# Two heads' score products issued in turn, their two PSUM banks held as one tile, in an attention, MoE and MLP kernel

## The chip, the cores and the metric

The kernel runs on one core of one Trainium2 chip. The metric is the device time of one execution in microseconds (us). The core has a matrix engine (TensorE, "PE" in the profile; its weight loads are listed apart as "PEld"), a vector engine (DVE), a scalar engine (ACT), GpSimd (POOL), and DMA queues that SyncE (SP) feeds.

## The reference

Causal attention with a decay goes into a mixture of four dense experts and then into an MLP with a gate.

```python
# q, k, v: (2, 8, 576, 64), f: (2, 8, 576)
scores = scale * np.matmul(q, k.transpose(0, 1, 3, 2))
cum = np.cumsum(np.log(np.clip(f, 0.0001, 1.0)), axis=-1)
scores = np.where(causal, -1e9, scores + cum[:, :, :, None] - cum[:, :, None, :])
attn = softmax(scores)                       # max, exp, sum + 1e-9
x = (attn @ v), laid out as (1152, 512)
# MoE: D = 512, E = 4, F = 1024
out += p[:, e:e + 1] * (np.maximum(x @ w1[e], 0.0) @ w2[e])   # for each e
# MLP: d_ff = 2048
h = x @ w_in
return (h * sigmoid(1.702 * h)) @ w_out
```

## The kernel before

The 1152 tokens (2 batches of 576) are cut into four chunks for the attention: 256 and 320 tokens of batch 0 (chunks 0 and 1), the same of batch 1 (chunks 2 and 3). Twelve weight blocks follow, eight of the MoE and four of the MLP. Every block is two layers (`emit_l1`, `emit_l2`, the `m` products in the traces). Nearly every product is made three times, from a rounded high part and a remainder: high by high, low by high, high by low.

The attention is cut into units, and a unit passes through scores (PE), maximum (DVE), exponential (ACT), division by the sum (DVE and POOL), transposes (PE, tile `t`), product with the values (PE, tile `x`). `emit_scores` makes the scores, and there are three kinds:

- "Plain" units, chunk 0 alone: one head, two query tiles, each one product of 65 rows (`s<-kd,qd`). There are 8 units with 16 tiles in all.
- Pair units: the same 128 queries of two heads. Head 0 lies in partitions 0 to 63 and head 1 in partitions 64 to 127 of the same tiles, so a product of either contracts over 64 rows (form `64*128` in the profile). Each head has three products and a PSUM bank of its own. There are 24 such units, of 128, 256, 384 or 512 keys.
- The tail units, 64 queries of both heads stacked over all 128 rows and 576 keys in two halves of 288: 8 units, two banks each.

The scores go into the PSUM pool `ps_s`, which holds two tiles of one bank each. `emit_max` (line 420) reads them on DVE, one or two instructions for each bank, and a bank comes free when its last reading is done. `ps_t` (three banks) holds `t` and `x`, `ps_m` (three banks) the layers' products; together they fill the eight banks.

The order of the instructions on an engine is fixed when the kernel is built: a scheduler works through the program by priorities and an estimate of time, and each engine then runs its list in that order. `tc.keep_in_program_order(ins)` holds an instruction in the order in which the program gives it. The main loop alternates layers (`m`) with calls of `pull()`, which emit the attention by units. When the attention's buffers come free, `begin_late` opens the buffers into which the MLP's 64-bit weights are loaded (`mst`, line 192), and DVE converts them (`cvt`, `wf`, `cvd`, lines 212 to 228).

Of the kernel before, what the change touches and what calls it, by code (L numbers as in the profile page):

```python
# [7 lines left out]
F32 = mybir.dt.float32  # L8
# [4 lines left out]
PSUM = bass.MemoryType.PSUM  # L13
# [19 lines left out]
def attn_moe_mlp(ctx: ExitStack, tc: tile.TileContext, qk0, qk1, qk2, v0, vp, fg, dp, wa_moe, wb_moe, wa_mlp, wb_mlp, outT):  # L33
# [6 lines left out]
    nc = tc.nc  # L40

    def pool(name, bufs, space=None, scope=ctx):
        kw = {} if space is None else {"space": space}
        return scope.enter_context(tc.tile_pool(name=name, bufs=bufs, **kw))
# [35 lines left out]
    att_scope = ctx.enter_context(ExitStack())  # L80
# [17 lines left out]
        p = late["ps"] if late and ps_n[0] % 8 < 5 else ps_m  # L98
        return p.tile([128, 512], F32, tag="m", name="m")

    ps_s = pool("ps_s", 2, PSUM, scope=att_scope)
    ps_t = pool("ps_t", 3, PSUM, scope=att_scope)

    tri = ac.tile([128, 128], F32, name="tri")
# [184 lines left out]
    def plain(c):  # L289


        return c == 0
# [74 lines left out]
    def emit_scores(c, u):  # L367


        hs, tiles = u  # L370
        out = []
        for q0 in tiles:
            w = min(q0 + 128, S)
            if plain(c):
                st = heads[c, hs[0]]
                mm = [(0, w, [(st["qd"][:, q0:q0 + 128], st["kd"][:, :w])])]
            else:
                p = pass_of[c]
                hi, lo = (pairs[p, hs[0]][k] for k in ("hi", "lo"))
                if q0 < 512:  # L380
                    o = S + 128 + q0 - p[2]
                    zs = [(0, w, slice(64 * g, 64 * g + 64)) for g in range(2)]
                else:
                    o = S
                    zs = [(a, z, slice(0, 128)) for a, z in ((0, 288), (288, S))]
                mm = [(a, z, [(l[r, o:o + 128], k[r, a:z]) for l, k in ((hi, hi), (lo, hi), (hi, lo))]) for a, z, r in zs]
            pts = []
            for a, z, _ in mm:
                pts.append(ps_s.tile([128, 512], F32, tag="s", name="s"))
                out.append((q0, w, a, z, pts[-1]))  # L390
            n = len(mm[0][2])
            for i in range(n):
                for pt, (a, z, lr) in zip(pts, mm):
                    nc.tensor.matmul(pt[:, :z - a], lhsT=lr[i][0], rhs=lr[i][1], start=i == 0, stop=i == n - 1)  # L394
        raw_s[c, u] = out

    def emit_max(c, u):
# [111 lines left out]
    def attention():  # L509
# [8 lines left out]
        first = {k: i for k, i in first.items() if k[0][2] or k[0][1]}  # L518
        nxt = list(first)
        per_unit = dict(scores=emit_scores, max=emit_max, exp=emit_exp, norm=emit_norm, tr=emit_tr)  # L520
        by_last = dict(pv=emit_pv, x2=emit_x2)
        names = sorted(STAGES, key=lambda k: -STAGES[k])
# [185 lines left out]
    for i, (kind, v_, b, c) in enumerate(seq):  # L708
# [6 lines left out]
        for g in range(4):  # L715
            ev = early[g] if i == 0 else (emit_l1 if kind == 1 else emit_l2)(v_, b, c, g)
            n = 0
            if nxt:
                j, cc = nxt[0]
                left = (j - i) * 4 - g  # L720
                n = max(0, -(-(due[cc] - pulled[0]) // left))
# [75 lines left out]
```

## Time and profile before

| what | us |
|---|---|
| median of three runs (736.33, 737.4, 1168.98) | 737.4 |
| the profiled execution, whole | 737.77 |
| its span, first to last instruction | 736.1 |
| PE busy, share of the span | 715.6, 97% |
| DVE busy | 460.2, 63% |
| ACT busy | 268.4, 36% |
| POOL busy | 277.6, 38% |

The profile is of one execution. A matmul's listed duration reaches from its start to a modelled end and overlaps with its successors, so what a matmul costs PE is read from start to start: in a timeline, the difference of the first column from one row to the next.

### The profile page before, as it was taken

To read this page: it belongs to the slowest core of one execution; us is meant where nothing else is said; L and a number is where in the kernel's file an instruction comes from. 1 tells how busy PE (TensorE), PEld (TensorE's weight loads), DVE (VectorE), ACT (ScalarE), POOL (GpSimd) and SP (SyncE) were. 2 spreads that over 40 slices of the span, in tenths; PEclk is the share of its full clock that TensorE was granted. 3 is DMA by queue.
4 is the path that set the end of the run, shared out by engine and by line. 5 is a ranking of instruction groups with operands and counts; after the bars stand their busy time and mean duration, and the time that the engine had idled before them with its cause. 6 is when DMAs were issued, how large, how long until landed. Compare 5 with 4: busy or idle time off the path is not lost.

```text
span 736.1 us, 11924 instructions
## 1 busy us (share of the span) xinstructions
PE 715.6 (97%) x4488; PEld 674.9 (92%) x4488; DVE 460.2 (63%) x1023; ACT 268.4 (36%) x629; POOL 277.6 (38%) x345
## 2 busy tenths in 40 slices
PE   4999999999999999999999999999999999999998
PEld 3576788888899999999998999999999999999997
DVE  4785666575758999999999633445972124424422
ACT  4564554566542233222211221223354433323420
POOL 4886974653432022233232433232462222222220
PEclk9999999999999999999999999999999999999999
DMA  8776534332216464464443301000100000000012
GB/s 290 222 233 208 159 123 132 90 103 86 73 51 216 144 194 149 148 183 117 130 144 115 86 24 35 1 1 1 58 0 1 1 1 1 1 0 1 1 44 86
DMA packets 29496, 67.23 MB, mean 91 GB/s; under 512 B 3032, under 2 KB 4576, under 8 KB 29440
## 3 DMA queue, kind: packets, MB, share of 16 engines
q1 hardware_dynamic: 29392, 66.44, 28.9%
q8 instruction: 35, 0.57, 0.3%
q14 instruction: 21, 0.17, 0.1%
q10 hardware_dynamic: 48, 0.05, 0.0%
HBM read 64.05 MB, written 2.41 MB: 90 GB/s over the span
## 4 chain that ended last, share of the span: by engine, by line
PE 75%; DVE 13%; DMA 5%; issue 3%; POOL 3%; ACT 0%; ACTq 0%; DVEq 0%; POOLq 0%
PE m L604 32%; PE m L560 31%; PE s L394 5%; PE t L461 3%; PE x L491 3%; DVE wlo L163 3%; DMA mst<-in_wa_mlp_dram 2%; DMA mst<-in_wb_mlp_dram 2%; DVE cvd L226 1%; DVE wf L220 1%; DVE cvt L214 1%; DVE tmp L618 1%; DVE cvt L212 1%; DVE hl L587 1%; DVE wf L228 1%
## 5 line engine op out<-in xcount | busy, mean ns | idle before, releaser
L620 POOL TENSOR_TENSOR acc<-acc,tmp 128x384 f32<-128x384 f32 (+3 forms) x112 | 111.2, 1004 | 248.9 <-DVE tmp L618 238.0
L604 PE MATMUL m<-hh,wlo 128*128 128x384 f32 (+2 forms) x640 | 128.0, 320 | 1.4 <-DVE wlo L163 1.3
L604 PE MATMUL m<-hh,whi 128*128 128x384 f32 (+2 forms) x640 | 129.1, 321 | 0.0
L604 PE MATMUL m<-hl,whi 128*128 128x384 f32 (+2 forms) x640 | 127.7, 320 | 0.0
L560 PE MATMUL m<-xh,whi 128*128 128x384 f32 (+2 forms) x624 | 126.1, 322 | 0.4 <-DVE hl L587 0.2
L560 PE MATMUL m<-xl,whi 128*128 128x384 f32 (+2 forms) x624 | 126.2, 321 | 0.0
L560 PE MATMUL m<-xh,wlo 128*128 128x384 f32 (+2 forms) x624 | 126.2, 321 | 0.0
L53 ACT ACTIVATE whi<-wst 128x512 fp32r<-128x512 f32 x103 | 64.9, 631 | 119.8 <-PE m L560 58.0
L163 DVE TENSOR_TENSOR wlo<-wst,whi 128x512 fp32r<-128x512 f32 x112 | 93.3, 836 | 24.3 <-ACT whi L53 13.7
L604 PEld LDWEIGHTS m<-hh,wlo 128*128 128x128 f32 x640 | 105.6, 188 | 3.2 <-DVE wlo L163 2.4
L604 PEld LDWEIGHTS m<-hh,whi 128*128 128x128 f32 x640 | 105.8, 188 | 1.7 <-issue 0.7
L560 PEld LDWEIGHTS m<-xh,whi 128*128 128x128 f32 x624 | 103.1, 188 | 3.7 <-issue 1.7
L604 PEld LDWEIGHTS m<-hl,whi 128*128 128x128 f32 x640 | 105.9, 188 | 0.8 <-issue 0.5
L560 PEld LDWEIGHTS m<-xl,whi 128*128 128x128 f32 x624 | 103.8, 188 | 0.9 <-issue 0.7
L560 PEld LDWEIGHTS m<-xh,wlo 128*128 128x128 f32 x624 | 103.7, 188 | 1.1 <-issue 1.0
L595 POOL TENSOR_TENSOR hl<-tmp,hh 128x384 fp32r<-128x384 f32 x48 | 49.1, 1025 | 133.3 <-ACT hh L53 133.3
L586 ACT ACTIVATE hh<-m 128x384 fp32r<-128x384 f32 (+2 forms) x112 | 48.9, 436 | 117.5 <-PE m L560 117.5
L587 DVE SCALAR_TENSOR_TENSOR hl<-m,hh 128x384 fp32r<-128x384 f32 (+2 forms) x112 | 54.9, 493 | 34.9 <-ACT hh L586 34.9
L618 DVE TENSOR_TENSOR tmp<-m,dpb 128x384 f32<-128x384 f32 (+2 forms) x80 | 40.9, 512 | 38.4 <-PE m L604 32.0
L593 DVE TENSOR_TENSOR tmp<-m,sg 128x384 f32<-128x384 f32 x48 | 26.6, 554 | 54.2 <-ACT sg L592 54.2
L443 POOL TENSOR_SCALAR e<-e,sm 128x128 f32<-128x128 f32 (+4 forms) x72 | 47.4, 668 | 29.4 <-DVE sm L441 15.7
L434 ACT ACTIVATE e<-e,mx 128x128 f32<-128x128 f32 (+4 forms) x72 | 41.9, 583 | 35.9 <-DVE mx L420 34.9
(80 smaller groups left out, 742.6 us busy)
## 6 DMA issues: line engine op xcount, KB each, us to landing
wst<-in_wa_moe_dram SPq DMA_DIRECT2D x28, 512.0 KB, 3.5
wst<-in_wb_moe_dram SPq DMA_DIRECT2D x28, 512.0 KB, 3.8
mst<-in_wa_mlp_dram SPq DMA_DIRECT2D x16, 512.0 KB, 3.5
mst<-in_wb_mlp_dram SPq DMA_DIRECT2D x16, 512.0 KB, 3.6
cb<-cumd SPq DMA_DIRECT2D x16, 256.0 KB, 4.1
vd<-in_vp_dram SPq DMA_DIRECT2D x8, 320.0 KB, 13.1
kq<-in_qk_dram SPq DMA_DIRECT2D x4, 608.0 KB, 7.2
cbs<-cumd SPq DMA_DIRECT2D x8, 288.0 KB
```

The source lines that it names most:

```text
L53: nc.scalar.activation(out=out, in_=in_, func=AF.Copy)
L163: sub = nc.vector.tensor_sub(lf, raw, f(hf))
L394: nc.tensor.matmul(pt[:, :z - a], lhsT=lr[i][0], rhs=lr[i][1], start=i == 0, stop=i == n - 1)
L434: nc.scalar.activation(out=e[:, off:off + w], in_=e[:, off:off + w], func=AF.Exp, scale=-1.0, bias=mx, accum_out=sm[:, 0, k:k + 1])
L443: nc.gpsimd.tensor_scalar(out=e[:, off:off + w], in0=e[:, off:off + w], scalar1=sm[:, 0, i:i + 1], scalar2=1.0, op0=ALU.mult, op1=ALU.mult)
L560: nc.tensor.matmul(p[:, :n], lhsT=w[:, k, :], rhs=x[c][:, k, :], start=(j == 0 and k == 0), stop=(j == 2 and k == 3))
L586: nc.scalar.activation(out=hh[:, g, :n], in_=p[:, :n], func=AF.Relu)
L587: nc.vector.scalar_tensor_tensor(out=hl[:, g, :n], in0=p[:, :n], scalar=0.0, in1=f(hh[:, g, :n]), op0=ALU.max, op1=ALU.subtract)
L595: nc.gpsimd.tensor_sub(hl[:, g, :n], t[:, :n], f(hh[:, g, :n]))
L604: nc.tensor.matmul(p[:, :n], lhsT=w[:, k, :], rhs=x[:, k, :n], start=(j == 0 and k == 0), stop=(j == 2 and k == 3))
L618: nc.vector.tensor_mul(t[:, :n], p[:, :n], d)
L620: nc.gpsimd.tensor_add(a, a, t[:, z])
```

## The change

The pool `ps_s` now holds one tile in place of two. `emit_scores` takes all banks of a query tile as one PSUM tile: two banks for pair and tail units, one for a plain tile. All of a unit's score products but the first are kept in program order, which is that of the loop: high by high of head 0, of head 1, low by high of head 0, of head 1, and so on. A plain tile has one product, so nothing is pinned there. The number of banks is the same.

```diff
-    ps_s = pool("ps_s", 2, PSUM, scope=att_scope)
+    ps_s = pool("ps_s", 1, PSUM, scope=att_scope)
...
-            for a, z, _ in mm:
-                pts.append(ps_s.tile([128, 512], F32, tag="s", name="s"))
+
+            ps = ps_s.tile([128, len(mm), 512], F32, tag="s", name="s")
+            for k, (a, z, _) in enumerate(mm):
+                pts.append(ps[:, k])
                 out.append((q0, w, a, z, pts[-1]))
             n = len(mm[0][2])
             for i in range(n):
                 for pt, (a, z, lr) in zip(pts, mm):
-                    nc.tensor.matmul(pt[:, :z - a], lhsT=lr[i][0], rhs=lr[i][1], start=i == 0, stop=i == n - 1)
+                    m = nc.tensor.matmul(pt[:, :z - a], lhsT=lr[i][0], rhs=lr[i][1], start=i == 0, stop=i == n - 1)
+                    if i or pt is not pts[0]:
+                        tc.keep_in_program_order(m)
```

The lines of the changed kernel lie two to four further down: its score products are line 396, its transposes 465, its value products 495, its layers 564 and 608.

PE's list in a pair unit of 512 keys in chunk 1, kernel before. `s` are scores, `khi` and `klo` the high and low parts of keys and queries, `m` a layer's products, `t` a transpose:

```order
L604 MATMUL m<-hh,wlo 128x256 x3
L394 MATMUL s<-khi 128x512 [waits DVE_49,PE_49]
L394 MATMUL s<-khi,klo 128x512
L394 MATMUL s<-klo,khi 128x512
L604 MATMUL m<-hh,wlo 128x256
L604 MATMUL m<-hl,whi 128x256 x3
L394 MATMUL s<-khi 128x512 [waits DVE_49,PE_49]
L394 MATMUL s<-khi,klo 128x512
L394 MATMUL s<-klo,khi 128x512
L461 MATMUL t<-identr,e 128x128 [waits Activation_49,Pool_49]
```

The same kind of unit on PE in the changed kernel:

```order
L564 MATMUL m<-xl,whi 128x256 x2
L396 MATMUL s<-khi 128x512 [waits DVE_49,PE_49]
L396 MATMUL s<-khi 128x512
L396 MATMUL s<-khi,klo 128x512 x2
L396 MATMUL s<-klo,khi 128x512 x2
L564 MATMUL m<-xl,whi 128x256 x2
```

The two heads' products, which stood in two groups of three with other work between, now stand as one group of six in which the heads alternate, and one wait on DVE takes the place of two.

PE's list at the start, with the plain tiles, kernel before:

```order
L394 MATMUL s<-kd,qd 128x256
L394 MATMUL s<-kd,qd 128x128 [waits DVE_49]
L394 MATMUL s<-kd,qd 128x256 [waits DVE_49]
L394 MATMUL s<-kd,qd 128x128 [waits DVE_49]
L461 MATMUL t<-identr,e 128x128 [waits Pool_49]
L394 MATMUL s<-kd,qd 128x256 [waits DVE_49]
L461 MATMUL t<-identr,e 128x128 [waits Pool_49]
L461 MATMUL t<-identr,e 128x128
L394 MATMUL s<-kd,qd 128x128 [waits DVE_49]
L394 MATMUL s<-kd,qd 128x256 [waits DVE_49]
```

The same start on PE in the changed kernel:

```order
L396 MATMUL s<-kd,qd 128x256 [waits DVE_49]
L396 MATMUL s<-kd,qd 128x128 [waits DVE_49]
L396 MATMUL s<-kd,qd 128x256 [waits DVE_49]
L465 MATMUL t<-identr,e 128x128 [waits Pool_49] x2
L465 MATMUL t<-identr,e 128x128
L396 MATMUL s<-kd,qd 128x128 [waits DVE_49]
L396 MATMUL s<-kd,qd 128x256 [waits DVE_49]
L465 MATMUL t<-identr,e 128x128 [waits Pool_49] x2
L465 MATMUL t<-identr,e 128x128
L495 MATMUL x<-ph,vd 64x256 [waits DMAHW3_49,PE_49]
```

Each plain tile now waits for DVE's reading of the tile just before it, and the first value product (`x`) stands behind six plain tiles in place of ten.

Three of the changed kernel's pair units are not one group on PE, this one of 128 keys among them:

```order
L396 MATMUL s<-khi 128x128 [waits DVE_49]
L465 MATMUL t<-identr,e 128x128 [waits Pool_49]
L465 MATMUL t<-identr,e 128x128 x3
L396 MATMUL s<-khi 128x128
L396 MATMUL s<-khi,klo 128x128 x2
L396 MATMUL s<-klo,khi 128x128 x2
```

The first product is not pinned to the rest, and four transposes have moved in behind it.

## Rows read from the trace of the kernel before

**Rows 1.** The page, busy us (share of the span) and instructions of PE.

```profile
PE 715.6 (97%) x4488; PEld 674.9 (92%) x4488; DVE 460.2 (63%) x1023; ACT 268.4 (36%) x629; POOL 277.6 (38%) x345
```

**Rows 2.** Windows: stretch, length, busy us of each engine, granted clock, DMA.

```profile
28.00:66.00 38.00, 36.62 (x236) 27.62 (x237) 27.03 (x86) 21.64 (x60) 31.16 (x49) 1.00 0.69 222
66.00:105.00 39.00, 35.93 (x263) 29.64 (x260) 24.48 (x74) 21.18 (x57) 29.61 (x39) 1.00 0.54 171
105.00:207.00 102.00, 101.88 (x712) 85.76 (x711) 66.45 (x204) 57.42 (x160) 50.37 (x74) 1.00 0.30 91
235.00:410.00 175.00, 173.41 (x1154) 171.61 (x1153) 170.18 (x324) 44.50 (x88) 46.60 (x43) 1.00 0.48 145
```

**Rows 3.** Waits of PE over the span: total us, times, longest.

```profile
PE s L394 <- DMA cumd<-fr: 10.1, 1, 10.1
PE s L394 <- DVE mx L420: 2.5, 2, 1.7
PE m L604 <- DVE wlo L163: 1.3, 2, 0.7
```

**Rows 4.** Timeline of PE, a 384-key unit with the heads in turn: start, us.

```profile
195.05 0.44 PE L394 MATMUL s<-khi 64*128 64x384 f32 x2
195.33 0.34 PE L394 MATMUL s<-khi,klo 64*128 64x384 f32 x2
195.50 0.33 PE L394 MATMUL s<-klo,khi 64*128 64x384 f32 x2
195.77 0.71 PE L604 MATMUL m<-hh,whi 128*128 128x320 f32 x3
```

**Rows 5.** Timeline of PE, units of 384, 128 and 512 keys with the heads apart.

```profile
42.16 0.44 PE L394 MATMUL s<-khi 64*128 64x384 f32 x1
...
42.88 0.55 PE L461 MATMUL t<-identr,e 128*128 128x128 f32 x3
...
155.33 0.33 PE L394 MATMUL s<-khi 64*128 64x128 f32 x1
...
155.81 0.56 PE L560 MATMUL m<-xl,whi 128*128 128x320 f32 x2
...
199.48 0.50 PE L394 MATMUL s<-khi 64*128 64x512 f32 x1
...
200.37 0.71 PE L560 MATMUL m<-xl,whi 128*128 128x320 f32 x3
201.01 0.50 PE L394 MATMUL s<-khi 64*128 64x512 f32 x1
...
201.90 0.85 PE L560 MATMUL m<-xh,whi 128*128 128x320 f32 x4
```

**Rows 6.** Chain of waits: 24 layer products of 320 columns in one piece.

```profile
210.16 3.52 PE m L604 x24
```

**Rows 7.** Tile `s` on PE: duration ns min/median/max, first and last start, forms.

```profile
L394 PE MATMUL s<-khi x64: 288/405/497, 27.9 to 205.8; 64*128 64x384 f32 x16, 64*128 64x512 f32 x16, 128*128 128x288 f32 x16, 64*128 64x128 f32 x8
L394 PE MATMUL s<-kd,qd x32: 273/421/795, 10.1 to 27.5; 65*128 65x128 f32 x16, 65*128 65x256 f32 x16
```

**Rows 8.** Timeline of all engines at the first plain tiles.

```profile
11.79 0.42 DVE L420 CUSTOM_DVE_ANT_0 e<-s,ones 128x256 f32<-128x256 f32 x1 [0.56 <-PE s L394]
...
12.27 1.35 PEld L394 LDWEIGHTS s<-kd,qd 65*128 65x128 f32 x4 [0.39 <-DVE mx L420]
```

**Rows 9.** DVE's readings of 512-key scores, by form: us, mean ns.

```profile
L420 DVE CUSTOM_DVE_ANT_0 e<-s,cb 128x512 f32<-128x512 f32 x16 | 10.8, 683 | 2.6 <-POOL e L443 1.4 <-PE s L394 1.2
```

**Rows 10.** Timeline: the last transposes, and the first load of MLP weights.

```profile
220.46 0.71 PE L461 MATMUL t<-identr,e 128*128 128x128 f32 x5
...
221.25 0.82 SPq L192 DMA_DIRECT2D mst<-in_wa_mlp_dram  x2
```

**Rows 11.** Chain of waits, where it leaves DVE for the last time.

```profile
405.03 1.42 DVE wlo L163
...
406.50 1.66 PE m L604 x8
```

## The prediction

> **What bounds the kernel now.** I read the page first: PE is busy for 715.6 us of the span of 736.1 [rows 1]. A listed duration overlaps its successors, so this alone doesn't prove that PE is full. The waits say more: PE waits 10.1 us at the start for the first data, and 2.5 us in two waits for DVE to read scores [rows 3]; 1.3 us for weight remainders is the next longest. The windows then say who is near PE in which stage [rows 2]. From 28 to 207 us, where the pair units stand, DVE has 118 of 179 us and POOL 111, so neither is full, though POOL has 30 of 39 us between 66 and 105. From 235 to 410 DVE has 170 of 175 us, the conversion of the MLP's weights, and the chain of waits leaves DVE for the last time at 406.5 [rows 11]. After that PE runs alone. So PE's own work sets the time almost everywhere, and a microsecond less of it in the attention counts wherever no other engine steps in.
>
> Last I read PE's timeline from start to start. Of the 24 pair units I counted five in which the scheduler has already put the heads in turn; the last one shows what this does [rows 4]. Six products of 384 columns take from 195.05 to 195.77, 0.72 us. With the heads apart, three products of one head take from 42.16 to 42.88, also 0.72 us [rows 5]. The two heads use different halves of the rows, and their products run at the same time: the second head is free when they alternate. When three products of one head follow each other, nothing runs beside them.
>
> **What the change removes.** A separated unit of 512 columns has two groups of 0.89 us (199.48 to 200.37 and 201.01 to 201.90) [rows 5], a pinned one should have one. Besides, every visit to 64-row products costs something before and after: the three layer products between the two groups take from 200.37 to 201.01, 0.64 us, where three in an undisturbed run take 3 x 3.52 / 24 = 0.44 [rows 6]. A visit costs 0.20 us.
>
> In the timeline from 27.9 to 205.8 us [rows 7] I find 14 units fully apart, the first at 27.9 and the last at 199.48:
>
> - seven of 512 keys: 7 x (0.89 + 0.20) = 7.6 us
> - four of 384: 4 x (0.72 + 0.20) = 3.7 us
> - two of 128 and one of 256: a group of 128 takes 155.33 to 155.81, 0.48 [rows 5]; the one of 256 lies between that and 0.72, I take 0.55. 2 x 0.68 + 0.75 = 2.1 us.
>
> Five more (one of 512, two of 384, one of 128 and one of 256) overlap in part. Whole, they would give 1.09 + 2 x 0.92 + 0.68 + 0.75 = 4.4 us; bounds 0 and 4.4, I take the half, 2.2. The five that are in turn already give nothing, and the tail units, which use all 128 rows, gain no overlap from the new order. Together 15.6 us. Three pair units of the changed kernel still lie in two pieces on PE, at 0.2 us for each extra visit: 0.6. This leaves 15.0 us of PE's work removed.
>
> **What it adds in the plain units.** Each of the 16 tiles now waits until DVE has read the one before. DVE's reading of 256 columns runs from 11.79 to 12.21, and the weight load that waited for it starts at 12.27 [rows 8], so a handover costs 0.06 us beyond the reading. Where a plain tile stands right behind another on PE, the reading of 0.42 us or less and two handovers come to about 0.5 us with PE idle. In PE's new list 7 of the 15 successions are of this kind; in the others a transpose or a value product lies between and covers the reading. 7 x 0.5 = 3.5 us. Bounds: 0, if the tiles were going to wait anyway for the units' chain through ACT and POOL, and 15 x 0.5 = 7.5. There are no layer products to fill the gap at that point, since the first `x` isn't made, and the transposes and value products behind the waiting tile wait with it.
>
> The first plain products run at half the pace of the last: the same forms have 421 ns as the median and 273 as the shortest [rows 7], and the timeline shows the short ones from 22.3 us on. The column of the granted clock says 1.00 in every window [rows 2], so I can only name it as a change of pace. A PE with more gaps may change later; for the work of that stretch I take 1 us, bounds 0 and 3.
>
> **What it adds in the pair and tail units.** A unit's first product waits until both banks of the unit before are read, and everything on PE behind it waits too. Before, each bank was waited for alone. DVE's reading of one head's 512 columns takes 0.68 us [rows 9], so both take 1.4. In the new list at least two microseconds of layer, transpose and value products (an estimate, by 0.147 us for a layer product of 320 columns [rows 6]) lie between two units, mostly four to six, so the reading is covered, if DVE comes to it at once. Before, such waits cost 2.5 us [rows 3]; I take the same sum again, so 0 added. Bounds: 2.5 less, and 36 units x 0.3 = 11 more, where DVE comes late each time.
>
> **What is moved.** The layers' products are the same on PE, and the last `x` comes after the same amount of them. The first load of MLP weights is issued at 221.25, right after the last transposes start at 220.46 [rows 10], because it needs their buffers. If the attention ends earlier, the loads and DVE's conversions start earlier by as much, and the stage that DVE fills moves as a whole. I put 0 there. The cover is PE's lead in that stage; where it is gone, PE waits as it does now just before 406.5, for 1.3 us in two waits [rows 3].
>
> The sum: 15.0 removed, 3.5 + 1 + 0 added, 10.5 us less. The profiled execution took 737.77, 1.7 us more than its span, and 0.4 more than the median of 737.4. 737.8 - 10.5 = 727.3, and I say 727.
>
> **Rivals.**
>
> The one tile is the bound (slower than before). Every pair and tail unit would show PE idle in front of its first score product, because DVE is busy with weight remainders (`wlo`) or evictions when the scores are done. It decides from (15.0 - 4.5) / 36 = 0.3 us for each unit; at 0.5 us it costs 18 us, and the time is 727.3 + 18 = 745. For it: one wait of this kind lasted 1.7 us already [rows 3]. Against it: DVE has a third of its time free from 28 to 207 us [rows 2], and the distance of the units. The Trainium skill, "TensorEngine Tiling (Array Packing)", section "Performance Considerations", speaks for this rival: packing speeds up TensorE but not the emptying of PSUM, which may become the bottleneck. By that rule the gain would be gone as in this rival; the trace so far has only the 2.5 us of waits on its side. Chance 0.07.
>
> POOL and DVE keep the pace from 66 to 105 us. In this stretch POOL makes the next pairs' high and low parts, and PE already shows 3 us of idle time [rows 2]. If PE is held there, the savings of the units in it are lost, about 0.92 + 1.09 + 0.7 + 0.92 = 3.6 us, and with a plain stage nearer to its upper bound the time is 730 to 735, say 732. Against it: the scheduler has moved more layer products ahead into this stretch, so PE has something to do. Chance 0.17.
>
> The stage that DVE fills takes the gain. If the conversions didn't move with PE, PE would meet them sooner and wait until the old time: about 736, and the change would not do what it says. Against it: the load behind the last transposes [rows 10]. Chance 0.04.
>
> Nothing is added. If the plain tiles wait anyway and the change of pace doesn't move, all 15 us remain: 722.8, and with the five half-overlapped units at the whole of 4.4 it is 720.6. Chance 0.16.
>
> The forecast, 723 to 731, has the remaining 0.56.
>
> **How the numbers follow.** A measurement of this kernel can tell about 2% from no change, 14.7 us: below 722.7 and above 752.1. Faster by over 2% is most of the case in which nothing is added: 0.15. Slower by over 2% needs the first rival at 0.7 us for each unit: 0.02. The rest, 0.83, lies within. The range is 720 to 735: it holds the forecast, the lossless case and the second rival, and leaves out the first and the third.
>
> **What would show it.** PE's timeline should show `s<-khi` rows by two in at least 21 of 24 pair units, six 512-column products within 0.9 us, and no group of three of one head. Between 10 and 30 us PE should show waits for DVE's `mx`, some 3 us in all, and the first pair unit should start 2 to 5 us later than 27.9. From then on PE should gain on the old kernel, and the last transposes should start near 210 in place of 220.5, with `mst` right behind, and the same 515 us from there to the end. The forecast is wrong if PE's waits for `mx` after 30 us come to more than 5 us, or if `mst` is issued earlier and the last piece of DVE in the chain is not.

## The result, and the profile after

The changed kernel took 744.25 us in the median (743.4 to 744.74, four runs), the kernel before 737.22 beside it; one of its four runs took 1168.98 us and does not count in the ratio. The ratio is 1.0083, with a 95% interval from 1.0061 to 1.0106: slower by about 6 us (7 by the medians), where 10 us less were forecast.

PE's row on the page, after. Busy time hardly moved from [rows 1]:

```profile
PE 714.9 (96%) x4488; PEld 674.6 (91%) x4488; DVE 453.0 (61%) x1023; ACT 267.9 (36%) x629; POOL 274.2 (37%) x345
```

PE's waits over the span, after (total us, times, longest):

```profile
PE t L465 <- POOL e L447: 9.0, 6, 2.9
PE s L396 <- DVE mx L424: 3.9, 7, 0.8
PE m L608 <- DVE wlo L163: 1.5, 3, 0.7
```

In [rows 3] PE's longest waits were for DVE's `mx`. Now it waits most for POOL's `e`, the division of the exponentials by their sum, which stood there with 0.8 us. All of the 3.9 us for `mx` lie before 46 us, and 6.7 of the 9.0 for `e` behind it.

The windows, after, with one more of 3.3 us (stretch, length, busy us, granted clock, DMA):

```profile
28.00:66.00 38.00, 34.53 (x176) 24.43 (x176) 21.27 (x75) 16.46 (x50) 21.13 (x36) 1.00 0.57 170
66.00:105.00 39.00, 35.23 (x268) 30.51 (x268) 24.87 (x75) 22.88 (x60) 24.04 (x36) 0.96 0.55 174
97.70:101.00 3.30, 3.30 (x16) 2.85 (x16) 1.48 (x8) 0.94 (x3) 3.30 (x6) 0.50 0.43 151
105.00:207.00 102.00, 99.37 (x735) 85.72 (x733) 64.75 (x211) 58.05 (x162) 60.36 (x87) 1.00 0.41 113
235.00:410.00 175.00, 174.13 (x1169) 172.94 (x1168) 169.42 (x328) 44.54 (x88) 45.66 (x43) 1.00 0.47 151
```

Against [rows 2], PE makes 176 products from 28 to 66 us where it made 236, and no engine there is busier than before. From 235 us on the rows are alike.

Where the time went shows in the score tile (PE, duration min/median/max in ns, first and last start):

```profile
L396 PE MATMUL s<-khi x64: 288/417/686, 45.7 to 220.4; 64*128 64x384 f32 x16, 64*128 64x512 f32 x16, 128*128 128x288 f32 x16, 64*128 64x128 f32 x8
...
L396 PE MATMUL s<-kd,qd x32: 421/606/797, 10.1 to 44.3; 65*128 65x128 f32 x16, 65*128 65x256 f32 x16
```

In [rows 7] the plain products ended at 27.5 and the pair products began at 27.9. Now they end at 44.3 and begin at 45.7. So 17.8 us were lost in the plain stage, and 8.0 by the first load of MLP weights (229.27 in place of 221.25, below). About 10 us were won back between, where the prediction had 15, and part of them is work that the plain stage had already taken ahead. The plain products never reach the fast pace of [rows 7]: their shortest is 421 ns, it was 273.

The pairing works. PE's timeline at a unit of 512 keys, after:

```profile
51.34 0.50 PE L396 MATMUL s<-khi 64*128 64x512 f32 x2
51.67 0.39 PE L396 MATMUL s<-khi,klo 64*128 64x512 f32 x2
51.90 0.40 PE L396 MATMUL s<-klo,khi 64*128 64x512 f32 x2
52.23 0.39 PE L585 MATMUL m<-xh,wlo 128*128 128x256 f32 x1
```

Six products take 0.89 us (51.34 to 52.23), as three of one head did in [rows 5]. Of the 24 pair units 21 stand so; three lie in two or three pieces.

The end of the attention, after (timeline, and the piece of the chain where it leaves DVE for the last time):

```profile
228.91 0.27 PE L465 MATMUL t<-identr,e 128*128 128x128 f32 x1
...
229.27 0.82 SPq L192 DMA_DIRECT2D mst<-in_wa_mlp_dram  x2
```

```profile
411.96 1.43 DVE wlo L163
413.39 0.04 issue
413.43 1.68 PE m L608 x8
```

The load stands right behind the last transposes, as in [rows 10], and the chain leaves DVE 6.9 us later than in [rows 11]. From the load to the end of the span are 743.0 - 229.3 = 513.7 us, before 736.1 - 221.3 = 514.8.

**How a plain tile goes round.** The timeline of all engines at the first plain tiles, after:

```profile
10.14 0.77 PE L396 MATMUL s<-kd,qd 65*128 65x128 f32 x2 [10.14 <-DMA kd<-fr]
10.94 0.29 DVE L424 CUSTOM_DVE_ANT_0 e<-s,ones 128x128 f32<-128x128 f32 x1 [4.81 <-PE s L396]
...
11.29 1.22 PE L396 MATMUL s<-kd,qd 65*128 65x256 f32 x2 [0.39 <-DVE mx L424]
...
12.55 0.42 DVE L424 CUSTOM_DVE_ANT_0 e<-s,ones 128x256 f32<-128x256 f32 x1 [1.31 <-PE s L396]
...
13.04 0.80 PE L396 MATMUL s<-kd,qd 65*128 65x128 f32 x2 [0.53 <-DVE mx L424]
```

Product, reading, product follow strictly. In the kernel before the first five tiles went on PE in one piece, so a product ran beside the reading of [rows 8]. PE's timeline there, before (a plain product stands in the profile as two instructions):

```profile
10.13 3.79 PE L394 MATMUL s<-kd,qd 65*128 65x128 f32 x10 [10.13 <-DMA cumd<-fr]
```

Over the 16 tiles I took the four parts of the round from such rows: from start to start a tile takes 2.24 us, before 1.14. Products and readings fill 1.3 of it. The rest is mostly six late returns, where 1.07 to 3.40 us pass between the reading and the next product. In these PE mostly works, on transposes and value products; it idles in two of them, 2.2 us together, for POOL's `e`. PE's timeline at the longest, after:

```profile
30.37 1.22 PE L396 MATMUL s<-kd,qd 65*128 65x256 f32 x2
31.52 1.54 PE L495 MATMUL x<-ph,vd 128*64 128x256 f32 x6
34.52 1.14 PE L465 MATMUL t<-identr,e 128*128 128x128 f32 x3 [1.46 <-POOL e L447]
35.45 0.64 PE L396 MATMUL s<-kd,qd 65*128 65x128 f32 x2
```

And POOL's in the same stretch:

```profile
28.43 0.45 POOL L349 TENSOR_TENSOR cb<-cb,tri 128x128 f32<-128x128 f32 x1
33.29 0.70 POOL L355 TENSOR_TENSOR cbs<-cbs,tri 64x64 f32<-64x64 f32 x2 [4.40 <-DMA cbs<-cumd]
34.09 0.82 POOL L447 TENSOR_SCALAR e<-e,sm 128x128 f32<-128x128 f32 x2
```

The next plain product stands in PE's list behind transposes, these wait for POOL's division, and the division stands in POOL's list behind the next pairs' mask addition, which waits 4.40 us for a load. In the kernel before a second tile was there, and the product could stand ahead of them.

### The profile page after: what moved, and what is told of

It reads as the page before. It is cut to its first block, busy times and chain, and to the rows that moved or that the text cites. A ratio compares the mean times of both kernels' runs of the same rounds, so it can differ in the third digit from the quotient of the medians.

```text
span 743.0 us, 11904 instructions
## 1 busy us (share of the span) xinstructions
PE 714.9 (96%) x4488; PEld 674.6 (91%) x4488; DVE 453.0 (61%) x1023; ACT 267.9 (36%) x629; POOL 274.2 (37%) x345
## 4 chain that ended last, share of the span: by engine, by line
PE 64%; DVE 17%; DMA 9%; issue 5%; POOL 4%; ACT 0%; POOLq 0%; DVEq 0%; SPq 0%
PE m L608 28%; PE m L564 26%; DMA mst<-in_wa_mlp_dram 4%; PE s L396 4%; DVE wlo L163 3%; PE t L465 3%; PE x L495 3%; DMA mst<-in_wb_mlp_dram 2%; DVE cvd L226 2%; DVE hl L591 2%; DVE cvt L212 2%; DVE wf L220 2%; DVE cvt L214 1%; DVE tmp L622 1%; DMA cb<-cumd 1%
## 5 line engine op out<-in xcount | busy, mean ns | idle before, releaser
L163 DVE TENSOR_TENSOR wlo<-wst,whi 128x512 fp32r<-128x512 f32 x112 | 95.0, 850 | 22.9 <-ACT whi L53 14.5
L447 POOL TENSOR_SCALAR e<-e,sm 128x128 f32<-128x128 f32 (+4 forms) x72 | 45.0, 635 | 34.8 <-DVE sm L445 17.9
```

The lines of the kernel that those rows point to most:

```text
L163: sub = nc.vector.tensor_sub(lf, raw, f(hf))
L447: nc.gpsimd.tensor_scalar(out=e[:, off:off + w], in0=e[:, off:off + w], scalar1=sm[:, 0, i:i + 1], scalar2=1.0, op0=ALU.mult, op1=ALU.mult)
```

## The experiments

The predictions on record speak of theories. A: PE's half pace up to 50 us is what costs. B: the one tile's own rounds in the plain stage. C: the later units. D came with the ninth run: POOL's list. "Before" medians beside them were 737.7 to 738.6; each ratio is to those of its own session, and differences between kernels of two sessions go by their ratios. A ratio isn't the quotient of the medians; the two lie up to 0.35% apart (`e3_plain_two`), so a difference of 2 or 3 us between kernels is not a firm one. Brackets hold the 95% interval of the ratio.

**Which half of the change does it?** `e1_pin_only` keeps the two one-bank tiles and pins the order:

```diff
                 for pt, (a, z, lr) in zip(pts, mm):
-                    nc.tensor.matmul(...)
+                    m = nc.tensor.matmul(...)
+                    if i or pt is not pts[0]:
+                        tc.keep_in_program_order(m)
```

> The pin alone: two one-bank score tiles as in the kernel before, with the products of a unit kept in the order of the loop, heads in turn. Theory A (TensorE's half pace lasted until 50.0 us in the changed kernel in place of 22.0, because single-tile plain units leave it idle too often, and that ate the saving): the plain stage is that of before, the pace rises near 22 us, and of the 15 us most remain: 722 to 728. Theory B (the idle time of the waits itself, with the pace a side matter): the same here, 722 to 728. Theory C (the units after the plain stage are at fault: PE held by POOL's division and DVE's readings there): the saving is lost here too, 733 to 740.

Measured: 736.77 us, 0.9978 [0.9951, 1.0005]. PE's timeline shows what pinning alone does:

```profile
42.02 0.44 PE L394 MATMUL s<-khi 64*128 64x384 f32 x1
42.39 0.55 PE L463 MATMUL t<-identr,e 128*128 128x128 f32 x3
42.69 0.36 PE L583 MATMUL m<-xh,whi 128*128 128x256 f32 x1
42.89 0.28 PE L583 MATMUL m<-xh,wlo 128*128 128x256 f32 x1
43.10 0.44 PE L394 MATMUL s<-khi 64*128 64x384 f32 x1
```

The first head's first product goes as soon as its own bank is free, and the other five wait for the second bank. So the heads overlap in part only: pair products take 25.9 us of PE from start to start, before 29.8, after 19.0. The time is in the band of theory C, but with most of the saving missing on PE itself it can't judge the theories.

`e2_tile_only` takes the joined tile and leaves out the pinning:

```diff
-                    if i or pt is not pts[0]:
-                        tc.keep_in_program_order(m)
```

> The tile alone: one tile of two banks, nothing pinned. Theory A: the pace rises near 50 us as in the changed kernel, and the heads' products lie apart more often: slower than the changed kernel by what pinning gives, 750 to 757. Theory B: the same sign, but only the waits of the plain stage: 741 to 746. Theory C: near the changed kernel, 742 to 747.

Measured: 744.84 us, 1.0071 [1.0038, 1.0104]. The time fits theories B and C. PE's list is the same, instruction for instruction, as in the changed kernel. The joined tile does the pairing, and the pinning does nothing beside it.

**The plain stage or the later units?** `e3_plain_two` gives the plain units two one-bank tiles in a pool of their own, and the later ones the joined tile:

```diff
+    ps_now = [pool("ps_p", 2, PSUM, scope=plain_scope), True]
+    def ps_scores(c, n):
+        if ps_now[1] and not plain(c):
+            plain_scope.close()
+            ps_now[:] = [pool("ps_s", 1, PSUM, scope=att_scope), False]
+        return ps_now[0].tile([128, n, 512], F32, tag="s", name="s")
```

> The changed kernel, except that the plain units have two tiles of one bank as before; the pool of one two-bank tile opens at the first pair unit. Theories A and B: the plain stage is that of before, the pace rises near 22 us, and 12 to 15 us come back against the changed kernel and more: 722 to 728. Theory C: the single two-bank tile holds PE in the later units, 735 to 742.

Measured: 736.02 us, 0.9940 [0.9909, 0.9971]. This is 1.4%, 10.5 us, under the changed kernel (1.0083) and only 0.6%, 4.4 us, under the one before: in the band of theory C, and over that of A and B. PE still waits 6.8 us for POOL's `e`. Nor is the plain stage wholly that of before, though it has its two tiles:

```profile
L403 PE MATMUL s<-kd,qd x32: 421/608/796, 11.6 to 31.7; 65*128 65x128 f32 x16, 65*128 65x256 f32 x16
```

The first product starts 1.5 us later, the shortest still takes 421 ns, and the fast pace comes at 39 us in place of 22. Part of what is missing to theories A and B may be this.

`e13_before_plain_one` is the counterpart: the kernel before, with one one-bank tile for the plain units alone (`pool("ps_p", 1, ...)`, and `ps_s` with two later).

> The kernel before in which the plain units alone have one one-bank score tile in place of two; pair and tail units as before on two, nothing joined or pinned. Theory B (with one tile each plain product waits for the reading of the one ahead, and the transposes that TensorE has between them lengthen the round): the last plain product starts after 40 us (27.5 in the kernel before) and the time is 8 to 12 us above the kernel before, 745 to 750. Theory C (the later joined tile is what costs, the plain stage is hidden by the rest): the plain stage may be longer, but the time stays within 3 us of the kernel before, 736 to 741.

Measured: 747.55 us, 1.0129 [1.0110, 1.0147], 9.5 us more. The tile `s` on PE:

```profile
L401 PE MATMUL s<-kd,qd x32: 421/606/797, 10.9 to 44.8; 65*128 65x128 f32 x16, 65*128 65x256 f32 x16
```

It is the changed kernel's plain stage, with nothing joined or pinned, and the time is the one that theory B gave. The two parts add up: 9.5 - 4.4 = 5.1 us, and the whole change measured 6.1.

This run is also the best control for the later units, since it differs from the changed kernel in these alone and the fast pace comes at 50 us in both. The joined tile is worth 0.46% there, 3.4 us (1.0129 to 1.0083; the intervals leave 1 to 6). PE's waits for POOL's `e`, over the span of this run (1.9 us of them before 47 us), and from 46 to 235 us in the changed kernel:

```profile
PE t L468 <- POOL e L450: 2.3, 3, 1.2
```

```profile
PE t L465 <- POOL e L447: 6.7, 4, 2.9
```

Pair and tail products take 36.9 us of PE in this run and 25.8 in the changed kernel, 11.1 less, and these waits are 6.3 more.

**Is it the pace?** In the changed kernel a plain product of 256 keys takes 1.22 us throughout, while the clock column reads 1.00. `e4_after_warm` puts 18 products of ones, whose result nobody uses, on PE ahead of the first scores; `e5_before_warm` does the same in the kernel before:

```diff
+    for i in range(18):
+        nc.tensor.matmul(wps, lhsT=wup[:, :128], rhs=wup, start=i == 0, stop=i == 17)
```

> The changed kernel with 18 products of a constant tile (128 by 512, bf16) on PE in the first 10 us, while PE waits for its first data; their PSUM tile isn't read. All waits of the plain stage stay. Theory A: if the full pace is reached before 10 us and kept, the work from 10 to 50 us runs at full pace and 8 to 14 us come back: 730 to 736. If the pace falls again in the plain stage's gaps, 740 to 744, and the row of the clock says when. Theory B: at most 3 us come back, 741 to 744, even with the full pace kept. Theory C: no change, 743 to 745.

> The kernel before with 18 products of a constant tile (128 by 512, bf16) on PE in the first 10 us; their PSUM tile isn't read. In the changed kernel with the same products the pace rose at 6.5 us and fell at 13.4, in the gaps of the plain stage. Theory A (the half pace in the plain stage costs what it lengthens, and PE's gaps bring it): here PE has hardly a gap from 10 to 22 us, so the full pace is kept, and up to half of that stretch is saved: 731 to 735. Theory B (the waits of the plain stage, not the pace): 735 to 738.

Measured: 743.10 us, 1.0053 [1.0023, 1.0083], and 741.92, 1.0042 [1.0012, 1.0071]. The first time fits theory B, and A with a pace that falls again. The second is over both bands, and slower than the kernel before. The fast pace didn't hold: in `e5_before_warm` the clock stood at 1.00 from 6.8 to 10.2 us and at 0.50 from there to 23.9, where PE idled 0.9 us in all. A window of the first of the two, and PE's timeline in it:

```profile
14.00:47.00 33.00, 28.64 (x89) 16.73 (x88) 18.95 (x68) 11.58 (x40) 21.20 (x43) 0.50 0.68 223
```

```profile
25.26 1.22 PE L401 MATMUL s<-kd,qd 65*128 65x256 f32 x2 [0.42 <-DVE mx L429]
27.00 0.80 PE L401 MATMUL s<-kd,qd 65*128 65x128 f32 x2 [0.31 <-DVE mx L429]
```

Here the column shows 0.50, which is 1.2 GHz, for the same 1.22 us. So 1.22 us is the half pace, and in the changed kernel the column's 1.00 in this stretch is no sign of the fast one.

`e6_after_fill` keeps PE fast by three more such products behind each plain tile; `e7_two_fill` is `e3_plain_two` with two behind each:

```diff
+    fill(18)
...
+            if plain(c):
+                fill(3)
```

> The changed kernel with 18 products of a constant tile in the first 10 us and three more behind each of the 16 plain tiles, in program order, so that PE has work while DVE reads; nothing reads them. Theory A: the pace is full from about 7 us on and stays so, the 12 us or so that the half pace adds come back, less what the fillers add: 731 to 738. Theory B (the waits): no better than the changed kernel, 743 to 750.

> The kernel with two one-bank tiles for the plain units and one pinned two-bank tile for the later ones, with 18 filler products in the first 10 us and two behind each plain tile. Theory A: the pace is full throughout, and most of the 15 us of the forecast appear: 722 to 728. Theory C (POOL's division comes too late for a PE that is ahead, and PE waits before transposes): the pace is full and still only 5 to 8 us are gained, 728 to 733, with waits for POOL's e of 5 us or more.

Measured: 743.96 us, 1.0074 [1.0046, 1.0101], and 741.24, 1.0016 [0.9982, 1.0050]. The first is in the band of theory B, the second over those of A and C. The pace did rise in the first of them (1.00 from 6.3 us on, but for 26.8 to 30.2):

```profile
20.56 0.70 PE L405 MATMUL s<-kd,qd 65*128 65x256 f32 x2
```

Yet its last plain product starts at 41.97 us. Up to the first pair unit the plain products, transposes and value products take 14.0 us of PE where they took 28.0, but the fillers take 12.3, and PE's idle time stays (6.5, in the changed kernel 6.2). Theory A as a cure falls. What the pace alone costs these runs don't tell, since the fillers cost nearly what it gave.

**POOL's division.** `e8_two_norm_dve` is `e3_plain_two` with the division of pair and tail units on DVE; `e10_before_norm_dve` makes the same move in the kernel before:

```diff
-            nc.gpsimd.tensor_scalar(out=e[:, off:off + w], ...
+            (nc.gpsimd if plain(c) else nc.vector).tensor_scalar(out=e[:, off:off + w], ...
```

> The kernel with two one-bank tiles for the plain units and one pinned two-bank tile for the later ones (736.0 us, PE waited 6.8 us for POOL's e before transposes), with the division of the later units on DVE in place of POOL. Theory C: PE's waits before transposes fall to 2 us or less, and the time to 729 to 733. Theory A alone: POOL's waits were not on the path, 734 to 738. If DVE becomes the bound instead, PE waits for DVE's mx or hl, and 735 to 742.

> The kernel before (two one-bank tiles, nothing pinned) with the division of pair and tail units on VectorE. It is the control for the version with the plain units on two tiles, one joined tile later and this division on VectorE (731.6 us). Theory D (the division's place matters only beside the joined tile, whose rounds wait for it): 735 to 739 us, no difference from the kernel before. The rival that the moved division by itself is the gain: 729 to 733 us.

Measured: 731.55 us, 0.9899 [0.9857, 0.9941], and 741.40, 1.0034 [1.0000, 1.0069], over the band of theory D. PE's waits in the first:

```profile
PE s L403 <- DVE mx L431: 5.6, 2, 5.1
PE t L473 <- POOL e L454: 1.8, 2, 1.4
```

The waits for POOL fell as theory C said, but DVE is late in its place once, by 5.1 us. The move is worth 0.4% to a kernel with the joined tile (0.9940 to 0.9899; these intervals overlap) and is no gain in the kernel without it. With the division on DVE the joined tile is worth 1.35% (1.0034 to 0.9899), about 10 us; with it on POOL 0.6%, or 0.46% by `e13_before_plain_one`. How much of this difference is the division's place isn't shown: in the profiles of `e3_plain_two` and `e10_before_norm_dve` the fast pace came at 39 and 37 us, in that of `e8_two_norm_dve` at 22, and both make the difference larger.

`e9_after_norm_dve` and `e11_two_norm_dve_all` move the division of every unit, in the changed kernel and in `e3_plain_two`:

> The changed kernel with the division of every unit, plain ones too, on VectorE and none on GpSimd. Theory D (in the changed kernel GpSimd's in-order list has the next pairs' mask additions, which wait for loads, and the key splits ahead of the plain units' divisions, and TensorE's transposes wait for these): the last plain product ends by 34 us (44.3 in the changed kernel, 27.5 before), TensorE's waits for the division's line sum to under 3 us, time 728 to 736. Theory B (the one tile's own round from product through reading and back is what spreads the plain units): the last plain product still ends after 38 us, and the time is 738 to 744.

> Plain units on two one-bank tiles, later units on one joined tile in pinned order, and the division of every unit on VectorE. Theory D: GpSimd's list holds no division any more, so that TensorE waits for none; the last plain product ends by 28 us and the time is 727 to 732. Rival: VectorE, which in the plain stage also reads the scores, takes over GpSimd's part as the one waited for: the last plain product ends after 30 us and the time is 733 to 738.

Measured: 741.30 us, 1.0049 [1.0027, 1.0070], and 729.80, 0.9889 [0.9862, 0.9916]. The first shows the tile `s` as before the move, and other waits (here up to 46 us):

```profile
PE s L396 <- DVE mx L424: 5.2, 8, 1.6
PE m L585 <- POOL whi L50: 2.0, 1, 2.0
```

```profile
L396 PE MATMUL s<-kd,qd x32: 415/582/796, 10.1 to 44.4; 65*128 65x128 f32 x16, 65*128 65x256 f32 x16
```

With no division on POOL the plain stage ends at 44.4 all the same, so for the plain stage theory D falls and B stands: PE's waits for `e` on POOL are gone, those for `mx` grew from 3.9 to 5.2 us (to 9.7 over the span), and 2.0 for POOL's `whi` are new. The two kernels differ by 11.5 us in the plain units' tiles alone. In the second the last plain product starts at 32.0 us, not by 28, but the time is in the band of theory D.

`e12_after_cb_dve` leaves the division and moves the mask additions, `cb` and `cbs`, from POOL to DVE in the changed kernel (`nc.gpsimd.tensor_add` to `nc.vector.tensor_add`, three lines).

> The changed kernel with the additions of the triangular mask to the loaded prefix rows on VectorE, and the division left on GpSimd. Theory D in its narrow form (the divisions stand behind additions that wait for a load): TensorE's waits for the division's line fall from 9.0 to under 4 us and the time is 732 to 740, unless VectorE's own list now stands behind the same loads, which would show as waits of VectorE for those loads of over 5 us before 235 us and a time of 740 to 750. Theory B: the division is not the cause; the last plain product ends after 40 us and the time is 742 to 746.

Measured: 787.37 us, 1.0671 [1.0641, 1.0700], far over every band. DVE's waits up to 235 us:

```profile
DVE cbs L355 <- DMA cbs<-cumd: 42.9, 7, 7.0
```

DVE reads the scores, and now stands 43 us behind loads. The run doesn't tell the theories apart; it shows what such waits cost on the engine that reads the scores. On POOL, in the changed kernel, the waits for `cbs` come to 20.0 us.

`e14_best_cum_queue` is `e11_two_norm_dve_all` with the loads of `cb` and `cbs` on ACT's queue (`nc.sync.dma_start` to `nc.scalar.dma_start`).

> The version with plain units on two tiles, one joined tile in pinned order later and every division on VectorE (729.8 us), with the loads of the prefix rows issued from ScalarE's queue in place of SyncE's. Theory D (GpSimd's waits for these loads, some 50 us of it up to 235 us, delay the key splits and so the products): the waits fall under 25 us and the time is 721 to 727. Rival (GpSimd has no division in its list any more and its waits lie beside other work): the time stays at 728 to 733, whatever becomes of these waits.

Measured: 740.61 us, 1.0044 [1.0027, 1.0061]. The time is over both bands, and the waits didn't fall as theory D supposed:

```profile
POOL cbs L362 <- DMA cbs<-cumd: 34.2, 8, 8.1
...
POOL cb L353 <- DMA cb<-cumd: 10.8, 3, 8.0
```

They come to 45 us, in `e11_two_norm_dve_all` to 52, and one of 4.6 us, until 38.7, lets PE wait 6.0 for a weight part that POOL makes behind it (`whi`). What these waits cost stays open.

**The number of rounds.** `e15_after_plain_joined` is the changed kernel, with both tiles of a plain unit in the two banks of the joined tile: 8 rounds in place of 16. `e16_joined_norm_dve` adds the division of every unit on DVE:

```diff
-            ps = ps_s.tile([128, len(mm), 512], F32, tag="s", name="s")
-            for k, (a, z, _) in enumerate(mm):
+            if not (plain(c) and out):
+                ps = ps_s.tile([128, 2, 512], F32, tag="s", name="s")
+            for k, (a, z, _) in enumerate(mm, len(out) if plain(c) else 0):
```

> The changed kernel in which the two score tiles of a plain unit (128 and 256 keys) lie in the two banks of the one joined tile, so that the plain stage takes 8 rounds of it in place of 16; everything else as in the changed kernel. Theory B (each of the 15 handovers costs the reading and what TensorE has between two products): the last plain product starts between 30 and 37 us (44.3 in the changed kernel) and the time is 736 to 740. Rival (one tile of any kind keeps the units from overlapping and TensorE at half pace): the last plain product starts after 40 us and the time is 742 to 746.

> As the run before, with the division of every unit on VectorE. Theory B with theory D (the division on GpSimd holds TensorE only where the rounds of the joined tile wait for it): 729 to 734 us, as with two plain tiles (729.8). Rival (VectorE, with division and reading both in the eight rounds, is late as it was with one tile per product): 738 to 742.

Measured: 733.79 us, 0.9933 [0.9907, 0.9960], and 729.18, 0.9889 [0.9843, 0.9934]. The tile `s` and PE's timeline in the first:

```profile
L397 PE MATMUL s<-kd,qd x32: 417/607/635, 10.3 to 32.8; 65*128 65x128 f32 x16, 65*128 65x256 f32 x16
```

```profile
10.26 1.62 PE L397 MATMUL s<-kd,qd 65*128 65x128 f32 x4 [10.26 <-DMA kd<-fr]
12.73 1.65 PE L397 MATMUL s<-kd,qd 65*128 65x128 f32 x4 [0.84 <-DVE mx L425]
14.35 1.14 PE L466 MATMUL t<-identr,e 128*128 128x128 f32 x3
15.29 1.48 PE L397 MATMUL s<-kd,qd 65*128 65x128 f32 x4
```

Half the rounds take 11.5 us out of the plain stage and 1.5% (1.0083 to 0.9933), 11 us, out of the time, with one tile and at the half pace still (median 607 ns). The time is 2 us under the band of theory B, the last product within it: theory B holds for the plain stage. The fast pace came at 39 us here, not 50, and its part in the 11 us isn't known. The second is, with `e11_two_norm_dve_all`, the fastest version found, 1.1% under the kernel before.

## Why the prediction was wrong

- **What bounds the kernel.** That PE's own work sets the time held from the pair units on. It didn't hold in the plain stage of the changed kernel: there the engines go round one after the other, and no busy share shows it.
- **15.0 us removed.** Right in mechanism. Pair and tail products take 37.4 us of PE from start to start before, 25.8 after and 25.2 in `e11_two_norm_dve_all`: 11.6 to 12.2 less. Of the forecast, 12.3 were the products themselves (6.2 + 2.9 + 1.5, and 1.7 for the half of the five); the other 2.7 were the price of the visits. Of these the traces show some: a layer product right before or behind a visit takes 0.06 to 0.08 us longer than one among layer products (0.120 at 256 columns, 0.147 at 320), 70 stand so before and 50 after, and together that is 1.6 us less.
- **3.5 + 1 us in the plain units.** This step failed. It measured 9.5 us (`e13_before_plain_one`), over the 7.5 that bounded the waits, and inside only with the 3 that bounded the pace. The 7 successions where one product follows another cost what the prediction charged: PE waits seven times for `mx`, 3.9 us. It charged nothing for the 8 where "a transpose or a value product lies between and covers the reading". The reading is covered there, but the tile's round isn't: in six of them the next product stands behind more work than the reading takes, and starts 1.07 to 3.40 us after it. Up to the first pair unit, the 17.8 us more are 4.5 in plain products, 2.7 in transposes, 3.7 in value products, 1.4 in layer products and 5.5 idle. Six transposes, eight value products and the layer products are work that would otherwise come later, some 5.6 us by the mean of each kind (an estimate). This leaves the 5.5 idle and 6.7 by which the same products took longer.
- **The change of pace** was 1 us, at most 3. The plain products stayed at the half pace to the end, and the first pair unit too. The 6.7 us are this and the missing overlap of neighbouring products together; the runs don't separate the two, nor the price of the pace from that of the rounds.
- **0 in the pair and tail units.** This failed too, and it is the larger part of the miss. The reading of the two banks is covered, as was said: PE waits for no `mx` behind 46 us, where it waited 2.5. But the step looked at DVE alone. PE waits 6.7 us there for POOL's division, and with the plain stage alike (`e13_before_plain_one` against the changed kernel) 3.4 us of time are left of 11.1 us of PE's work; by `e3_plain_two` it is 4.4. The waits lie inside the bound of 11, on another engine than the one named.
- **0 for the stage that DVE fills.** Right; it moved as a whole.
- **The rivals.** The first gave 745 and came nearest, but not by its mechanism: it put a wait for DVE in front of all pair and tail units, and there is none. (There are 24 + 8 = 32 of these and not 36, so by its own terms it gives 743, and the bound of 11 is 9.6.) Its title, one tile is the bound, is true of the plain units, to which it wasn't applied. The Trainium skill, "TensorEngine Tiling (Array Packing)", section "Performance Considerations", says that packing speeds up TensorE but not the emptying of PSUM, which may become the bottleneck after a speedup of 4. Here the speedup is 2, and the trace shows no such bottleneck in the packed units, with no wait for `mx`; where PE does wait for a reading, 3.9 us, the products aren't packed. The second rival, POOL and DVE keeping the pace from 66 to 105 us, named the right engine: PE waits 3.8 us there for POOL's division, and 2.6 behind 105 us.
- **What would show it.** The forecast asked for the first pair unit 2 to 5 us later; it is 17.8. This was the sign that failed, and it stands in the first row of the tile `s`. The waits for `mx` up to 30 us were near the 3 us asked for. Neither of the two signs named for a wrong forecast appeared: PE waits 0.7 us for `mx` behind 30 us, and `mst` isn't issued earlier. Both watched DVE, and the time was lost elsewhere.

With 9.5 in place of 4.5, and 4.4 won later in place of 15.0, the sum is 737.8 + 5.1 = 742.9, against 744.74 of the profiled execution. Of the 15.6 us between this sum and the forecast, 10.6 are the saving that didn't arrive, and 5.0 the plain units.

## What to carry to other kernels

When buffers are joined, look for whoever else takes from the same pool: here the pairing was for units with two banks, and units with one lost their second buffer. Price a buffer that is taken away by the whole round from one product to the next, through everything that the engine's list puts between, and not by the wait for the one reading. And where PE gets faster, look on every engine of the unit's chain at what stands ahead in its list, not at its busy share.

## What the runs showed of the hardware

The granted clock fell to 0.50 from 97.70 to 101.00 in the changed kernel, after PE had waited 2.86 us for POOL's `e` and gone on at 96.45. The kernel before had no such stretch between its plain units and the end of its layers. In the plain stage the fast pace came at 22 us in the kernel before and near 50 with one tile, and 18 products ahead of it brought it from 6.5 to 13.4 us only. But it also came as late as 39 us (`e3_plain_two`) and 37 us (`e10_before_norm_dve`) with two tiles, where PE idles 0.4 and 0.1 us between its first product and the first pair unit, against 0.7 in the kernel before; idle time alone doesn't tell these runs apart.
